# One core, linear attention and two gated layers: 160 orders from the planner, and leftover output sums moved amid the last up-projections

## The chip, the cores and the metric

The kernel runs on one core of one Trainium2 chip. The metric is device time in microseconds (us) of one execution; the lower, the better. The engines are called as in the profile: PE (TensorE), DVE (VectorE), ACT (ScalarE), POOL (GpSimd), SP (the engine whose queue issues the transfers).

## The reference

```
# attention: q, k, v are 4 batches x 8 heads x 576 rows x 64
q_s = softmax(q, over the 64)
k_s = softmax(k, over the 576 rows)
kv  = einsum('bhsd,bhse->bhde', k_s, v)
x   = einsum('bhsd,bhde->bhse', q_s, kv)      # then 2304 rows x 512
# layer 0 (2304 x 512, width 1536)
x = (silu(x @ w_gate) * (x @ w_val)) @ w_out
# layer 1, same sizes
out = ((x @ w_a) * (x @ w_b)) @ w_out2
```

All in float32. The kernel keeps that precision by splitting each operand of a product into a rounded high half and a low remainder and making three products (low x high, high x low, high x high) where the reference has one.

## The kernel before

**Stages.** In the first 140 us the attention of batches 0 and 1 runs together with layer 0 for the first block of 512 rows (block 0); the layer's twelve weight slices w_0 to w_11 are brought in and converted meanwhile (`convert`: the instructions of lines 390 to 416 on ACT, DVE and POOL, then a high half `w<-a` on ACT, line 416, and a low half `w<-a` on DVE or POOL, line 304). For slice f, PE makes 24 up-projection matmuls (`u_0_f`, line 837), and later 12 down-projections (`acc`, line 864) of the slice before. Attention works in units of two heads. A unit's matmuls on PE are `kx` (line 647) and `kb` (652), which take the maximum of the keys over the rows and spread it, `kv` (710, 711), `qt` (758), `ql` (761), `xt` (771) and `xl` (781); around them DVE finds maxima (`kr`, 650) and subtracts (`ut<-ut,kb`), ACT takes exponentials and copies `qt` to SBUF (765). Up to 293 us follows block 1 with the attention of batches 2 and 3, and from there the rest of both layers in three supersteps of six `step`s, which use a scheme in the manner of Strassen: seven products of half size in place of eight.

**A step** makes up-projections `p` (line 1115, six matmuls each, in `begin`, `middle` and `end` for m = 0 and 1), copies and gates their results (ACT lines 1127, 1131, 1153; DVE `temps<-p`), splits the gated tiles into `hs` (names hp and l2w in the rows, since they share those buffers), and makes output chunks `o` (`out_chunk`, lines 1226 and 1228, six matmuls each), whose results DVE adds into `sums`. Steps of the supersteps 0 and 2 also have the rows left over from the blocks: `rest_up` (`q`, line 1199, four results a step) and two more chunks, o_8 and o_9, added into `rs`. A step's chunks are not made in the step itself; they are `left` for the next. There, two of them go amid the m = 1 up-projections (in the loop with `end(1, which)`) and the others behind the `q` matmuls. The last step's own ten chunks come at the very end. The output weights of a step are split from `raww` into `outs_w` (`make_out`, ACT and DVE or POOL, lines 311 and 304). In the supersteps with rest rows this pair of buffers is the same in each step, so the split waits until the last chunk of the step before has been multiplied.

**The order.** No engine program is written by hand. `add` records every operation with its engines, cost in us, buffers and dependences. `prepare` gives each operation a due time, backwards from its successors, and `order` is a list scheduler: it takes the operation that can start first by its model of the engines, among those the one with the smallest due time, also picks DVE or POOL (or ACT or DVE) where an operation may go to either, and sets `self.length` to the end of its plan. `emit` then issues everything in that order, engine by engine; on the chip each engine keeps this order and waits in it. `soon` adds a chunk and gives its additions an early due time.

Of the kernel before, what the change touches and what calls it, by code (L numbers as in the profile page):

```python
# [1 line left out]

# [14 lines left out]
class Buf:  # L17
# [3 lines left out]
    def __init__(self, pool, shape, dtype, tag, name):  # L21
        self.pool, self.shape, self.dtype, self.tag, self.name = pool, shape, dtype, tag, name
        self.tile, self.users, self.seen, self.free = None, [], {}, False
# [7 lines left out]
class Plan:  # L31
# [13 lines left out]
    TABLE = 1.3  # L45
    WINDOW = 10.24 / 3
    FAR = 1e9

    def __init__(self):
        self.ops, self.last, self.rank = [], {}, {}  # L50
# [44 lines left out]
    def prepare(self):  # L95
# [7 lines left out]
        for n in reversed(range(len(ops))):  # L103
            op = ops[n]
            cost = op["cost"] + op["nbytes"] / self.DMA_RATE
            lands = (self.DMA_START + self.DMA_END) * (op["nbytes"] > 0)
            t = self.FAR
            for s in self.succ[n]:
# [9 lines left out]
    def order(self):  # L118
# [10 lines left out]
        def free_at(tag):  # L129
            if tag not in holder:  # L130
                return 0.0
            users = holder[tag].users
            return max(end[u] for u in users) + self.HOP if all(u in end for u in users) else self.FAR

# [6 lines left out]
        def port_at(n, engine):  # L141

            return max(port_free if e == engine and port else 0.0 for e, _, _, port in ops[n]["runs"])

        def better_here(n, r):

            (engine, cost, *_), (here, cost_here, *_) = ops[n]["runs"]
            queue = ready[engine]
            ahead = sum(ops[o]["cost"] for o in queue if due[o] < due[n] and queue[o] <= r + 1)
            return max(free.get(here, self.BEGIN), r, port_at(n, here)) + cost_here <= \  # L150
                max(free.get(engine, self.BEGIN), r, port_at(n, engine)) + ahead + cost
# [4 lines left out]
        while len(done) < len(ops):  # L156
            best = None
            for engine, queue in ready.items():
                options = []
                for n, r in queue.items():  # L160
# [3 lines left out]
                    for b in ops[n]["allocs"]:  # L164
                        r = max(r, min(free_at(tag) for tag in b.tag))
                    if r < self.FAR and (ops[n]["engine"] == engine or better_here(n, r)):
                        options.append((max(r, port_at(n, engine)), n))
# [44 lines left out]
        self.length = max(end.values())  # L212
        return done, run, slot

    def emit(self):
        self.prepare()
        done, run, slot = self.order()
        for b, tag in slot.items():
            b.tag = tag
        for n in done:  # L220
            self.ops[n]["runs"][run[n]][2]()
# [3 lines left out]
def kernel(  # L225
# [108 lines left out]
    NP = NF // 2  # L334
# [635 lines left out]
    def unit(u):  # L970
# [27 lines left out]
    SUMS = [((sums, k), lambda k=k: sums()[:, k]) for k in range(2 * R)] + \  # L998
        [((b, 0), lambda b=b: b()) for b in rest_sums]
    BANKS = ("at0", "at1", "acc2", "acc3")  # L1000
    SOON, SOONER, KEEP = 2.0, -30.0, 6
    main["soon"] = SOON
    SUPER = [(0, (2, 3), True, 512), (1, (0, 1), False, 512), (1, (2, 3), True, 512)]

    def bank(name):
        return Buf(pg, [P, 512], F32, BANKS, name)

    def parts(s):

        RAW, (l, blocks, _, width) = [*RAW1, *RAW2[s]] if s else [*RAW2[0], *RAW1], SUPER[s]  # L1010

        def cols(x):
            return x().rearrange("p (c n) -> p c n", c=2)[:, :, 0:width]

        for q, (t, h) in enumerate(((0, 0), (0, 1), (1, 0), (1, 1))):
            i = blocks[t]
            pieces = [(i, 0, width, 0)] if i < B else [(i - 1, width, SM - width, 0), (i, 0, B * SL, SM - width)]
            for src, at, size, to in pieces:
                last_x[:] = [dma(lambda q=q, h=h, src=src, at=at, size=size, to=to: nc.sync.dma_start(
                    out=RAW[q][1]().rearrange("p (c n) -> p c n", c=2)[:, :, to:to + size],  # L1020
                    in_=xd[l][src]()[:, 2 * h:2 * h + 2, at:at + size]),
                    P * 2 * size * 4, [(xd[l][src], (2 * h + c, 0)) for c in range(2)] if s == 0 else [xd[l][src]],
                    [(RAW[q][0][0], (RAW[q][0][1], to))], after=[*last_x, *(() if s or t == 0 else pair_buf["after"])])]

        def keys(q):
            return [(RAW[q][0][0], (RAW[q][0][1], to)) for to in ((0, SM - width) if blocks[q // 2] == B else (0,))]

        def halve(o, q):
            (hi_key, hi), (lo_key, lo) = ops_x[o]
            split(lambda: cols(hi), lambda: cols(lo), lambda: cols(RAW[q][1]), 2 * width, hi_key, lo_key, keys(q))  # L1030

        def less(q, x, y, op=ALU.subtract):
            pair(2 * width, lambda: cols(RAW[q][1]), lambda: cols(RAW[x][1]), lambda: cols(RAW[y][1]), op,
                 [*keys(x), *keys(y)], keys(q))

        halve(0, 0)
        less(0, 0, 2)
        less(2, 2, 3, ALU.add)
        halve(2, 2)
        halve(4, 0)  # L1040
        less(0, 3, 0)
        halve(1, 0)
        halve(3, 1)
        less(1, 1, 0)
        halve(5, 3)
        halve(6, 1)

    def rest_parts(l):
        last_x[:] = [dma(lambda: nc.sync.dma_start(
            out=RAW1[0][1]().rearrange("p (c n) -> p c n", c=KD), in_=xd[l][B]()),  # L1050
            P * PART * 4, [xd[l][B]], [(RAW1[0][0][0], (RAW1[0][0][1], 0))], after=[*last_x, *pair_buf["after"]])]
        (hi_key, hi), (lo_key, lo) = rest_x
        split(hi, lo, RAW1[0][1], PART, hi_key, lo_key, (RAW1[0][0][0], (RAW1[0][0][1], 0)))

    def step(s, j):
# [91 lines left out]

        p = [[Buf(pg, [P, 512], F32, (f"gv{m}",) if x == 1 else BANKS, f"p{n}_{m}_{x}") for x in range(3)] for m in range(2)]
        A, Bt = T
# [129 lines left out]
    def soon(chunk):  # L1279
        start = len(plan.ops)  # L1280
        chunk()
        for n in range(start, len(plan.ops)):
            if plan.ops[n]["engine"] in ("vector", "scalar"):
                plan.rank[n] = main["at"] + SOONER

    left, later = [], []
    for s, (l, _, rested, _) in enumerate(SUPER):
        parts(s)
        if rested:
            rest_parts(l)  # L1290
        for j in range(NP):
            begin, middle, end, rest_up, chunks, make_out = step(s, j)
            begin(0)
            while j == 0 and len(left) > KEEP:
                soon(left.pop(0))
            middle(0)
            begin(1)
            end(0, 0)
            end(0, 1)
            middle(1)  # L1300
            for which in range(2):
                if left:
                    soon(left.pop(0))
                end(1, which)
            for i in range(2 * rested):
                rest_up(i)
            for c in left:
                soon(c)
            for halve in later:
                halve()  # L1310
            later.clear()
            make_out()
            left = chunks
# [35 lines left out]
```

## Time and profile before

| | |
|---|---|
| median of 3 runs | 957.19 us (956.98 to 959.25) |
| profiled execution | 957.91 us, its span 955.5 us, mean granted PE clock 0.990 |
| busy share of the span | PE 96%, DVE 67%, ACT 54%, POOL 34% |

The span reaches from the first to the last instruction in the profile; the profiled execution's time is 2.4 us longer. PE is busy for 916.6 us of the span, and the other engines have room on average. A share of the span hides that the stages differ, so the stretches are read one by one.

### The profile page before, as it was taken

The page shows a single profiled execution, that of the slowest core. Times are in us where ns is not written, and L with a number is a line of the kernel's source. Part 1 is how long each engine was busy: PE and PEld are TensorE (multiplying, and loading weights), DVE is VectorE, ACT ScalarE, POOL GpSimd, SP SyncE. Part 2 cuts the span into 40 slices and gives each one's busy share as a digit, 9 for nine tenths or more (in the row PEclk, how much of TensorE's full clock was granted, in tenths as well). Part 3 has the DMA queues.
Part 4 walks back from the last instruction along what each step waited for, and adds up shares of the span by engine and source line. Part 5 has one row for each costly group of instructions (what it writes and reads, how often), then busy time and mean ns, then how long its engine had stood idle before and what let it go on. Part 6 is the DMA issues. An engine that isn't in the chain of part 4 may idle for free.

```text
span 955.5 us, 12768 instructions
## 1 busy us (share of the span) xinstructions
PE 916.6 (96%) x4400; PEld 755.8 (79%) x4400; DVE 641.9 (67%) x1029; ACT 519.2 (54%) x1020; POOL 325.2 (34%) x321
## 2 busy tenths in 40 slices
PE   5689899999999999999999999999999999999997
PEld 3477687877887888888888888888777888888885
DVE  7899897445377887867878775765686444564444
ACT  4797975877765665455454456443643453433311
POOL 6513211111124422343456333353464213242210
PEclk9899899999999999999999999999999999999999
DMA  9949675364337444453432652422223210110003
GB/s 269 290 165 283 216 223 188 115 193 123 84 102 254 131 134 153 130 157 122 143 111 69 207 188 88 135 90 84 67 65 108 83 44 23 45 45 23 23 1 110
DMA packets 108151, 121.41 MB, mean 127 GB/s; under 512 B 31928, under 2 KB 83896, under 8 KB 107960
## 3 DMA queue, kind: packets, MB, share of 16 engines
q1 hardware_dynamic: 102424, 116.55, 38.8%
q10 hardware_dynamic: 5664, 4.07, 1.4%
q8 instruction: 34, 0.56, 0.2%
q14 instruction: 29, 0.24, 0.1%
HBM read 88.60 MB, written 31.98 MB: 126 GB/s over the span
## 4 chain that ended last, share of the span: by engine, by line
PE 85%; DVE 6%; DMA 3%; ACT 2%; issue 2%; POOL 1%; SPq 1%; ACTq 0%; DVEq 0%; POOLq 0%
PE p L1115 34%; PE o L1226 14%; PE u L837 12%; PE q L1199 7%; PE o L1228 6%; PE acc L864 6%; PE o L1236 2%; DVE l2w L304 2%; PE kv L710 1%; DVE sums L304 1%; PE xt L771 1%; PE u L822 1%; DMA r<-x 1%; DMA wr<-in_moe_w_gate_dram 1%; DMA raw<-x 1%
## 5 line engine op out<-in xcount | busy, mean ns | idle before, releaser
L1115 PE MATMUL p<-l2w,l2w 128*128 128x512 f32 x1512 | 353.6, 390 | 3.2 <-ACT temps L1127 1.5
L1115 PEld LDWEIGHTS p<-l2w,l2w 128*128 128x128 f32 x1512 | 282.7, 188 | 64.8 <-DVE temps L304 2.9
L837 PE MATMUL u<-xhl,w 128*128 128x512 f32 x552 | 147.7, 414 | 3.9 <-DVE w L304 3.9
L837 PEld LDWEIGHTS u<-xhl,w 128*128 128x128 f32 x552 | 104.1, 195 | 29.5 <-DVE w L304 4.9
L311 ACT CAST l2w<-raww 128x512 fp32r<-128x512 f32 x144 | 88.2, 620 | 66.8 <-PE p L1115 35.2
L304 DVE TENSOR_TENSOR sums<-o,sums 128x512 f32<-128x512 f32 x120 | 82.2, 688 | 53.6 <-PE o L1226 38.4
L304 POOL TENSOR_TENSOR l2w<-raww,l2w 128x512 fp32r<-128x512 f32 x56 | 76.7, 1375 | 94.6 <-ACT l2w L311 92.8
L304 DVE TENSOR_TENSOR temps<-p,temps 128x512 f32<-128x512 f32 x90 | 62.1, 690 | 64.1 <-PE p L1115 63.3
L304 DVE TENSOR_TENSOR l2w<-raww,l2w 128x512 fp32r<-128x512 f32 x88 | 71.2, 820 | 31.8 <-ACT l2w L311 31.7
L1226 PE MATMUL o<-l2w,hp 128*128 128x512 f32 x288 | 82.4, 395 | 2.9 <-DVE sums L304 1.5
L864 PE MATMUL acc<-h,w 128*128 128x512 f32 x288 | 73.9, 400 | 0.0
L1127 ACT COPY temps<-p 128x512 f32<-128x512 f32 x72 | 42.4, 588 | 57.9 <-PE p L1115 57.3
L1226 PEld LDWEIGHTS o<-l2w,hp 128*128 128x128 f32 x288 | 53.3, 188 | 16.1 <-DVE sums L304 3.2
L1199 PE MATMUL q<-rest,l2w 128*128 128x256 f32 x432 | 65.4, 283 | 0.0
L864 PEld LDWEIGHTS acc<-h,w 128*128 128x128 f32 x288 | 52.9, 188 | 12.8 <-issue 0.8
L1199 PEld LDWEIGHTS q<-rest,l2w 128*128 128x128 f32 x432 | 58.6, 192 | 0.9
L311 ACT CAST l2w<-temps 128x512 fp32r<-128x512 f32 x36 | 22.3, 621 | 62.9 <-PE o L1226 47.8
L1226 PE MATMUL o<-l2w 128*128 128x512 f32 x192 | 54.6, 392 | 0.0
L304 POOL TENSOR_TENSOR raww<-raww,spare 128x512 f32<-128x512 f32 x15 | 20.8, 1385 | 86.1 <-DVE l2w L304 86.0
L1226 PE MATMUL o<-l2w,l2w 128*128 128x512 f32 x168 | 44.6, 391 | 0.0
L1228 PE MATMUL o<-hp,l2w 128*128 128x512 f32 x144 | 41.9, 399 | 1.3 <-DVE sums L304 1.2
L1226 PEld LDWEIGHTS o<-l2w 128*128 128x128 f32 x192 | 36.0, 188 | 8.3
(197 smaller groups left out, 1482.3 us busy)
## 6 DMA issues: line engine op xcount, KB each, us to landing
raww<-wf SPq DMA_DIRECT2D x36, 512.0 KB, 4.0
raww<-wf SPq DMA_DIRECT2D x36, 256.0 KB, 2.7
wf<-latewr SPq DMA_DIRECT2D x36, 256.0 KB, 3.1
wf<-a SPq DMA_DIRECT2D x16, 384.0 KB, 2.8
latewr<-in_moe_w_a_dram SPq DMA_DIRECT2D x24, 256.0 KB, 3.7
latewr<-in_moe_w_b_dram SPq DMA_DIRECT2D x24, 256.0 KB, 4.8
latewr<-in_moe_w_out_dram SPq DMA_DIRECT2D x12, 512.0 KB, 4.3
wr<-in_moe_w_gate_dram SPq DMA_DIRECT2D x22, 256.0 KB, 4.9
```

The lines of the kernel that those rows point to most:

```text
L304: engine.tensor_tensor(out=out(), in0=x(), in1=y(), op=op)
L311: add("scalar", act_us(n), lambda: nc.scalar.copy(out=hi(), in_=src()), src_keys, [hi_key])
L710: nc.tensor.matmul(pk(), lhsT=kx()[:, r, :], rhs=vx()[:, :, r, :], start=(r == 0), stop=False)
L771: add("tensor", 0.95, lambda: nc.tensor.matmul(px(), lhsT=kvbd(), rhs=qT()[:, 0:SM], start=True, stop=True), [QT, *BDS], [px], due=due)
L837: nc.tensor.matmul(ps()[:, 0:n], lhsT=wv[:, c, :], rhs=x()[:, xs, c, 0:n], start=(a == 0 and c == 0), stop=(a == 2 and c == KD - 1))
L864: nc.tensor.matmul(ps()[:, 0:n], lhsT=w()[:, 4 + ws, o * P:(o + 1) * P], rhs=h()[:, hs, 0:n], start=begin, stop=end)
L1115: nc.tensor.matmul(ps()[:, 0:width], lhsT=wv(o)[:, m, ws, c, :], rhs=ops_x[o][xs][1]().rearrange("p (c n) -> p c n", c=2)[:, c, 0:width], ...
L1127: add("scalar", act_us(n), lambda: nc.scalar.copy(out=to[1]()[:, 0:n], in_=ps()[:, 0:n]), [ps], [to[0]], due=main["at"] + main["soon"])
L1199: nc.tensor.matmul(ps[m]()[:, 0:256], lhsT=wv(o)[:, m, ws, c % 2, :], rhs=rest_x[xs][1]().rearrange("p (c n) -> p c n", c=KD)[:, c, :], st ...
L1226: nc.tensor.matmul(ps(), lhsT=lhs(i, hs), rhs=outs_w[i][1]()[:, ws * 512:(ws + 1) * 512], **ends)
L1228: nc.tensor.matmul(ps()[:, 0:width], lhsT=outs_w[i][1]()[:, ws * 512 + r * P:ws * 512 + (r + 1) * P], rhs=hs2[i][t][1]()[:, hs * 512:hs * ...
L1236: nc.tensor.matmul(ps()[:, o * 256:(o + 1) * 256], lhsT=outs_w[i][1]()[:, ws * 512 + at:ws * 512 + at + P], rhs=rest_h[1]()[:, (2 * i + hs ...
```

## The change

`search` runs `order` 160 times. From the second time on it first moves 3% of the due times by up to 3 us either way, and it keeps the moved due times where the plan's length does not grow. `emit` issues the last order kept. In the last step of superstep 2 (`EARLY[2]` is 1), chunks that were left over from the step before are added right behind `end(0, 0)` until four are left, and behind `end(0, 1)` until two are left; those two go in the loop as before, so none is left for behind the `q` matmuls.

```
+    ROUNDS = 160
+    def search(self):
+        self.prepare()
+        rng, best = random.Random(0), None
+        for n in range(self.ROUNDS):
+            kept = self.due
+            if best:
+                self.due = [d + rng.uniform(-3, 3) if rng.random() < 0.03 else d for d in kept]
+            try:
+                found = self.order()
+            except RuntimeError:
+                self.due = kept
+                continue
+            if best and self.length > best[0]:
+                self.due = kept
+            else:
+                best = self.length, found
+        return best[1]
...
     def emit(self):
-        self.prepare()
-        done, run, slot = self.order()
+        done, run, slot = self.search()
...
+    EARLY = (0, 0, 1)
...
             end(0, 0)
+            early = EARLY[s] if j == NP - 1 else 0
+            while early and len(left) > 4:
+                soon(left.pop(0))
             end(0, 1)
+            while early and len(left) > 2 * (early < 2):
+                soon(left.pop(0))
             middle(1)
```

In the rows of the changed program, lines stand 20 to 21 higher than before up to 1226 (304 is 324, 837 is 857, 1115 is 1136, 1226 is 1247).

**The last step, on PE.** Before, behind o16_0 (the first chunk left over from the step before) PE goes on like this, and only then to the `q` of the last step, number 17:

```order
L1226 MATMUL o16_0_7577<-l2w10_2926 128x512 x3
L1115 MATMUL p17_1_1_7540<-l2w5_2608,l2w8_2639 128x512 x6
L1226 MATMUL o16_1_7593<-l2w9_2686,hp0_2906 128x512 x3
L1226 MATMUL o16_1_7593<-l2w10_2926 128x512 x3
L1115 MATMUL p17_1_2_7533<-l2w6_2694,l2w8_2639 128x512 x6
L1199 MATMUL q17_0_0_7608<-rest2_2714,l2w9_2686 128x256 x2
L1199 MATMUL q17_0_0_7608<-rest2_2714,l2w7_2565 128x256 x2
```

Now the last chunks left over stand there:

```order
L1247 MATMUL o16_8_7642<-l2w9_2685,l2w6_2698 128x512 x3
L1247 MATMUL o16_8_7642<-l2w10_2919,l2w6_2698 128x512 x3
L1136 MATMUL p17_1_1_7540<-l2w5_2613,l2w8_2627 128x512 x6
L1247 MATMUL o16_9_7659<-l2w9_2685,l2w6_2698 128x512 x3
L1247 MATMUL o16_9_7659<-l2w10_2919,l2w6_2698 128x512 x3
L1136 MATMUL p17_1_2_7533<-l2w6_2698,l2w8_2627 128x512 x6
L1220 MATMUL q17_0_0_7680<-rest2_2719,l2w9_2685 128x256 x2
L1220 MATMUL q17_0_0_7680<-rest2_2719,l2w7_2565 128x256 x2
```

Eight chunks have moved from behind the 48 `q` matmuls to ahead of them. Behind the last `q` the step's own chunks now follow at once:

```order
L1220 MATMUL q17_1_1_7728<-rest2_2719 128x256 x2
L1220 MATMUL q17_1_1_7728<-rest2_2719,l2w8_2627 128x256 x2
L1220 MATMUL q17_1_1_7728<-rest2_2719 128x256 x2
L1220 MATMUL q17_1_1_7728<-rest2_2719,l2w8_2627 128x256 x2
L1247 MATMUL o17_0_7743<-l2w9_2685,hp0_2897 128x512 x3
L1247 MATMUL o17_0_7743<-l2w10_2919 128x512 x3
```

**The last step, on ACT.** Before, these are its last instructions but two; `l2w9` and `l2w10` from `raww` are the high halves of the last step's output weights, `tr` is the gate of `q`:

```order
L1127 COPY temps_2800<-p17_1_1_7540 128x512
L1131 ACTIVATE tr_2963<-q17_0_0_7608 128x256
L1131 ACTIVATE tr_2963<-q17_1_0_7637 128x256
L311 CAST hp0_2906<-tc_2822 128x512
L311 CAST l2w10_2926<-temps_2800 128x512 x2
L311 CAST hp1_2946<-temps_2800 128x512
L311 CAST l2w9_2686<-raww_1910 128x512
L311 CAST l2w10_2926<-raww_1910 128x512
```

Now the same instructions stand in this order:

```order
L331 CAST hp0_2897<-tc_2818 128x512
L331 CAST l2w10_2919<-temps_2798 128x512
L331 CAST hp1_2941<-temps_2798 128x512
L331 CAST l2w9_2685<-raww_1907 128x512
L331 CAST l2w10_2919<-raww_1907 128x512
L1152 ACTIVATE tr_2957<-q17_0_0_7680 128x256
L331 CAST l2w10_2919<-temps_2798 128x512
```

The casts of hp0, l2w10, hp1 and of the output weights (`<-raww`) have moved ahead of the first `tr<-q`.

**The first step of superstep 2, on ACT.** Before, the cast of the rest rows (`rest2<-r1`, whose rows arrive by a transfer) stands ahead of the gate and of the copy of `p12_1_1`, for which PE's next up-projection waits:

```order
L1127 COPY temps_2800<-p12_1_2_6148 128x512
L311 CAST rest2_2714<-r1_2538 128x1024
L1131 ACTIVATE temps_2800<-p12_0_1_6082 128x512
L311 CAST l2w8_2639<-raww_1910 128x2x256
L311 CAST l2w9_2686<-raww_1910 128x2x256
L1127 COPY temps_2800<-p12_1_1_6155 128x512
```

Now:

```order
L1148 COPY temps_2798<-p12_1_2_6147 128x512
L1152 ACTIVATE temps_2798<-p12_0_1_6083 128x512
L331 CAST rest2_2719<-r1_2538 128x1024
L331 CAST l2w8_2627<-raww_1907 128x2x256
L1148 COPY temps_2798<-p12_1_1_6154 128x512
```

The gate `temps<-p12_0_1` has moved ahead of the cast of the rest rows, and one of the two casts of `raww` behind the copy of `p12_1_1`.

**Block 0, on PE, around slice 6.** Before, unit 6's `kb` and unit 7's `kx` stand between the down-projections and the up-projections of slice 7:

```order
L864 MATMUL acc0_2_550<-h0_0_5_984,w0_5_810 128x512 x3
L864 MATMUL acc0_3_556<-h0_0_5_984,w0_5_810 128x512 x3
L652 MATMUL kb6_1059<-ident_78,kr6_1004 128x128
L647 MATMUL kx7_1078<-ident_78,tm7_1018 128x128 x2
L647 MATMUL kx7_1078<-ident_78,ut7_829 128x128
L837 MATMUL u0_0_7_0_1089<-xhl0_0_286,w0_7_1036 128x512 x12
L837 MATMUL u0_0_7_1_1128<-xhl0_0_286,w0_7_1036 128x512 x12
```

Now unit 6's `kx` and `kb` come ahead of slice 5's up-projections:

```order
L667 MATMUL kx6_876<-ident_78,tm6_823 128x128 x2
L667 MATMUL kx6_876<-ident_78,ut6_702 128x128
L730 MATMUL kv5_886<-ut5_473 128x130 x4
L731 MATMUL kv5_886<-ut5_473 128x130
L672 MATMUL kb6_897<-ident_78,kr6_892 128x128
L857 MATMUL u0_0_5_0_913<-xhl0_0_299,w0_5_835 128x512 x12
```

And between slices 6 and 7 there is no attention any more:

```order
L884 MATMUL acc0_0_550<-h0_0_5_995,w0_5_835 128x512 x3
L884 MATMUL acc0_1_558<-h0_0_5_995,w0_5_835 128x512 x3
L884 MATMUL acc0_2_564<-h0_0_5_995,w0_5_835 128x512 x3
L884 MATMUL acc0_3_572<-h0_0_5_995,w0_5_835 128x512 x3
L857 MATMUL u0_0_7_0_1113<-xhl0_0_299,w0_7_1037 128x512 x12
L857 MATMUL u0_0_7_1_1131<-xhl0_0_299,w0_7_1037 128x512 x12
```

Two matmul groups of attention that stood right ahead of `u0_0_7` are gone from there.

**Block 0, on DVE, up to the second half of w_6.** Before, the low halves of w_6 are made here:

```order
L406 SCALAR_TENSOR_TENSOR a0_6_1_925<-wr0_6_1_812,a0_6_1_925 128x768
L411 ISA a0_6_1_925<-wr0_6_1_812,a0_6_1_925 128x1536
L304 TENSOR_TENSOR w0_6_953<-a0_6_0_859,w0_6_953 128x3x256
L851 TENSOR_TENSOR u0_0_5_1_927<-s0_0_5_932,u0_0_5_1_927 128x512
L304 TENSOR_TENSOR w0_6_953<-a0_6_1_925,w0_6_953 128x3x256
L397 TENSOR_SCALAR a0_7_0_977<-a0_7_0_977 128x768
```

Now there is more between and ahead of them:

```order
L417 TENSOR_SCALAR a0_6_1_943<-a0_6_1_943 128x768
L324 TENSOR_TENSOR w0_6_959<-a0_6_0_884,w0_6_959 128x3x256
L420 TENSOR_SCALAR a0_6_1_943<-a0_6_1_943 128x768
L871 TENSOR_TENSOR u0_0_5_1_954<-s0_0_5_964,u0_0_5_1_954 128x512
L426 SCALAR_TENSOR_TENSOR a0_6_1_943<-wr0_6_1_825,a0_6_1_943 128x768
L431 ISA a0_6_1_943<-wr0_6_1_825,a0_6_1_943 128x1536
L417 TENSOR_SCALAR a0_7_0_990<-a0_7_0_990 128x768
L324 TENSOR_TENSOR h0_0_5_995<-u0_0_5_1_954,h0_0_5_995 128x512
L420 TENSOR_SCALAR a0_7_0_990<-a0_7_0_990 128x768
L735 TENSOR_SCALAR ks6_1017<-kv6_1002 128x2
L426 SCALAR_TENSOR_TENSOR a0_7_0_990<-wr0_7_0_908,a0_7_0_990 128x768
L324 TENSOR_TENSOR w0_6_959<-a0_6_1_943,w0_6_959 128x3x256
```

The second low half, `w0_6<-a0_6_1`, now stands behind work on slice 7, behind `h0_0_5` and, further ahead, behind unit 6's `kr6` and its two subtractions of `kb6` and behind `tm7`, all of which came after it before.

## Rows read from the trace of the kernel before

**Rows 1.** Windows: length, busy of PE, PEld, DVE, ACT, POOL, PE clock, DMA, GB/s

```profile
24.00:50.00 26.00, 18.41 (x76) 13.54 (x75) 22.76 (x36) 20.19 (x42) 14.02 (x18) 0.87 0.92 297
...
100.00:125.00 25.00, 21.81 (x88) 17.16 (x87) 21.02 (x35) 22.31 (x49) 7.90 (x7) 0.86 0.66 213
...
300.00:900.00 600.00, 594.05 (x2904) 497.87 (x2903) 403.13 (x600) 292.80 (x520) 234.31 (x166) 1.00 0.32 102
```

**Rows 2.** Timeline of PE, 88 to 126 us: start, duration, what, idle before

```profile
90.78 1.16 PE L710 MATMUL kv<-ut 128*128 128x130 f32 x8 [1.39 <-ACT ut L765]
...
101.65 5.74 PE L837 MATMUL u<-xhl,w 128*128 128x512 f32 x24
107.22 2.96 PE L864 MATMUL acc<-h,w 128*128 128x512 f32 x12
...
112.61 0.44 PE L647 MATMUL kx<-ident,tm 128*128 128x128 f32 x2 [2.31 <-DVE ut L304]
...
114.50 8.02 PE L837 MATMUL u<-xhl,w 128*128 128x512 f32 x22 [0.88 <-DVE w L304]
122.36 2.26 PE L864 MATMUL acc<-h,w 128*128 128x512 f32 x9
124.46 1.05 PE L710 MATMUL kv<-ut 128*128 128x130 f32 x8
```

**Rows 3.** Timeline of DVE, 100 to 113 us

```profile
100.03 0.95 DVE L304 TENSOR_TENSOR w<-a,w 128x768 fp32r<-128x768 f32 x1
100.90 0.55 DVE L397 TENSOR_SCALAR a<-a 128x768 f32<-128x768 f32 x1
101.37 0.68 DVE L304 TENSOR_TENSOR h<-u,h 128x512 fp32r<-128x512 f32 x1
101.97 0.55 DVE L400 TENSOR_SCALAR a<-a 128x768 uint32<-128x768 uint32 x1
102.44 0.55 DVE L650 TENSOR_REDUCE kr<-kx 128x1 f32<-128x384 f32 x1
102.91 0.94 DVE L406 SCALAR_TENSOR_TENSOR a<-wr,a 128x768 uint32<-128x768 uint32 x1
103.77 0.41 DVE L304 TENSOR_TENSOR tm<-ut 128x256 f32<-128x256 f32 x1
...
110.33 0.69 DVE L304 TENSOR_TENSOR ut<-ut,kb 128x512 f32<-128x512 f32 x1
...
112.27 0.28 DVE L304 TENSOR_TENSOR ut<-ut,kb 128x128 f32<-128x128 f32 x1
```

**Rows 4.** Timeline of PE at the first step of superstep 2

```profile
722.38 1.65 PE L1115 MATMUL p<-l2w,l2w 128*128 128x512 f32 x6 [1.49 <-ACT temps L1127]
```

**Rows 5.** Timeline of ACT at the same place

```profile
719.27 1.05 ACT L311 CAST rest<-r 128x1024 fp32r<-128x1024 f32 x1 [3.14 <-DMA r<-x]
720.22 0.59 ACT L1131 ACTIVATE temps<-p 128x512 f32<-128x512 f32 x1
...
721.74 0.58 ACT L1127 COPY temps<-p 128x512 f32<-128x512 f32 x1
```

**Rows 6.** Timeline of PE in the last step

```profile
918.39 3.04 PE L1199 MATMUL q<-rest,l2w 128*128 128x256 f32 x24
...
924.15 0.85 PE L1226 MATMUL o<-l2w,hp 128*128 128x512 f32 x3
...
936.76 0.97 PE L1226 MATMUL o<-l2w,hp 128*128 128x512 f32 x3 [1.38 <-DVE l2w L304]
```

**Rows 7.** Timeline of ACT in the last step

```profile
934.74 1.30 ACT L311 CAST l2w<-raww 128x512 fp32r<-128x512 f32 x2 [1.08 <-PE o L1226]
```

**Rows 8.** Timeline of DVE in the last step

```profile
936.03 1.28 DVE L304 TENSOR_TENSOR l2w<-raww,l2w 128x512 fp32r<-128x512 f32 x2
```

**Rows 9.** The page's groups of instructions: the same subtraction on POOL and DVE

```profile
L304 POOL TENSOR_TENSOR l2w<-raww,l2w 128x512 fp32r<-128x512 f32 x56 | 76.7, 1375 | 94.6 <-ACT l2w L311 92.8
...
L304 DVE TENSOR_TENSOR l2w<-raww,l2w 128x512 fp32r<-128x512 f32 x88 | 71.2, 820 | 31.8 <-ACT l2w L311 31.7
```

More of the change, by code (lines that the diff above doesn't have):

```diff
@@ L1 @@
+import random
 from contextlib import ExitStack
```

## The prediction

> **What bounds the kernel now.** I read the windows first. They give, for each stretch, how long each engine was busy, and the reader should compare PE's busy time with the stretch's length. From 300 to 900 us PE is busy for 594.05 of 600 us [rows 1]: PE sets the pace, and an edit there can win only single waits. From 24 to 50 us it is busy for 18.41 of 26 us, from 100 to 125 us for 21.81 of 25, and the granted clock is 0.87 and 0.86 there: part of the matmuls ran at 1.2 GHz instead of 2.4. In these stretches DVE is busy for 22.76 of 26 and 21.02 of 25 us. So the front is bound by the conversion of the weight slices on DVE and ACT, with PE waiting for it, and the rest is bound by PE.
>
> Then the timelines of PE, in which square brackets give the idle time before a row and what ended it. Three places can be touched by the change. In the front, PE waits 2.31 us for unit 7's `kx` and 0.88 us for the low half of w_7; the 22 matmuls behind take 8.02 us, 0.365 us each, where 24 like them took 5.74 us, 0.239 each [rows 2]. The difference, 22 x 0.126 = 2.8 us, is the low clock after the waits. At 722 us PE waits 1.49 us for a copy on ACT [rows 4]. At 936.76 it waits 1.38 us for the last step's output weights [rows 6].
>
> **The last step: -1.4 us.** The number of matmuls is the same; eight chunks are only moved ahead of `q`. Before, ACT could cast the output weights only at 934.74, behind the last leftover chunk, whose buffers they take [rows 7]; DVE took their low halves from 936.03 [rows 8], and PE waited 1.38 us. Now the leftover chunks end ahead of `q`, and `q` lasts from 918.39 to 924.15, 5.76 us [rows 6]. The two casts (1.30 us together) and two subtractions (1.28 on DVE, or 1.375 for the one that POOL now has [rows 9]) fit into it: at the worst one behind the other 1.30 + 1.28 + 1.38 = 4.0 us. All of the 1.38 us goes if nothing else is late. What is late next is the low half of the last gated tile: behind the last up-projection DVE has an addition and a multiplication, ACT a cast, DVE a subtraction, and in the new order the cast stands behind `tr<-q17_0_0`, the subtraction behind the multiplication for `q17_0_1`. `q17_0_1` is the second of four and ends half of `q` later, at 2.9 us; with some 0.7 us for each of the two DVE instructions behind it the low half is there at about 4.3 us, 1.5 us before it is needed. What the eight chunks displace in the up-projections is covered: each is 1.4 us of PE (924.15 to 936.76 less the wait is eight of them: 11.2 us) and leaves DVE one addition of 0.7 us. The ends are -1.4 and 0; I take -1.4.
>
> Beside it stands a row against that slack: the same subtraction takes 820 ns on DVE over 88 of them [rows 9], and 640 ns a piece in the pair at 936.03 [rows 8], so something stretches it in places. The Trainium skill, page "SBUF — State Buffer", section "Who interferes with whom", says that a DVE instruction with two SBUF inputs and a GpSimd instruction that reads SBUF lock each other out. The trace agrees in direction (a mean above the undisturbed pair); POOL has four such subtractions or products in the last step now, and by that rule the last low half could be up to one POOL instruction, 1.4 us, later, at 5.7 us against 5.8. That would still give -1.4 us, but with the slack gone; it is part of why the third rival below is not left out.
>
> **The first step of superstep 2: -0.8 us.** ACT waited for the transfer of the rest rows until 719.27, then ran their cast, 1.05 us, the gate, two casts and only at 721.74 the copy [rows 5]. PE had nothing to do from 722.38 - 1.49 = 720.89 [rows 4], when the copy's input was ready. Now the gate runs in ACT's wait for the transfer, and one cast of 0.6 us goes behind the copy. So the copy could start at 721.74 - 0.59 - 0.57 = 720.6; it starts when its input is there, at about 720.95, and 0.8 us is saved. Ends: 0 if the transfer lands later than before, -1.5 if the rest of the wait goes as well. I take -0.8.
>
> **The front: -0.5 us.** Around slice 6 the new orders of PE and DVE pull unit 6's `kx` and `kb` ahead of slice 5, and its `kv` ahead of slice 6. That has a price: the second half of w_6 on DVE now stands behind eight further instructions of some length. Six of them followed it directly before, from 100.90 to 104.18, 3.3 us; the two subtractions of `kb` are 0.69 and 0.28 [rows 3]. So w_6 is complete at 100.03 + 0.95 + 4.2 = 105.2, and `u0_6` starts there instead of at 101.65. If the clock stays high, it ends at 110.9, the 2.96 us of `acc` end at 113.9, and `u0_7` starts when w_7 is there. That came at 114.5 before [rows 2]; DVE has much the same work ahead of it, only in another order, and I put it at 115.0. Then `u0_7` takes 5.74 us at full clock, without the wait of 2.31 us for `kx`, and ends at 120.7; before, it ended at 122.36. That is -1.7 us. If the wait of 3 us ahead of `u0_6` lowers the clock, as it was low behind the waits at 112.61 and 114.50, 2.8 us are added there: 113.7, `acc` 116.7, `u0_7` 122.4, no change. Two more moves belong to this: `kv` of unit 6, 1.05 us at 124.46, now runs in the wait ahead of `u0_6`, and `xt` of unit 6 now stands right behind `qt` and `ql`, so that it waits for ACT's copy of `qt`; the nearest such wait is 1.39 us at 90.78 [rows 2]. Together +0.3. So -1.4 to +0.3; I take -0.5, near the middle. From there to 140 us both orders do the same slices, and I carry it on unchanged. Before slice 5 the new order moves DVE's and ACT's work too, to and fro; I have no row that tells which way it goes and put nothing there.
>
> **The rest: +0.5 us.** In block 1 and behind it, PE's rows are shuffled as well, mostly attention among up-projections, where PE has almost no idle time, so it can hardly gain. A `kb` moved nearer to its `kx` or a `kv` nearer to its `kb` makes a wait. The bounds are 0 and one wait of 2.31 us such as `kx` had [rows 2]. I take +0.5, nearer to 0, since most distances are kept.
>
> **Sum.** -0.5 + 0.5 - 0.8 - 1.4 = -2.2 us. The profiled execution took 957.91 us (span 955.5 and 2.4 us around it), so it would take 955.7, its span 953.3. It lies 0.7 us above the median of the runs; the same step from 957.19 gives 955.0 us.
>
> **Rivals.**
> - *The front gains in earnest.* For it speaks that PE lost 3.2 us of waits and 2.8 us of clock between 112 and 122 us, and that DVE itself is idle for 4 of the 25 us from 100 to 125 us [rows 1], so that w_6 and w_7 could come sooner than my count of rows says. If the front gained those 4.0 us, the sum is -4.0 + 0.5 - 0.8 - 1.4 = -5.7: 951.5 us by the median. Against it speaks the longer line ahead of w_6.
> - *Slower, by w_6.* If `u0_6` starts at 105.2 at the low clock and the clock stays low through all 24 matmuls and the 12 of `acc`, these take 24 x 0.365 + 12 x 0.365 = 13.1 us instead of 8.5; `u0_7` starts at 118.3 instead of 113.7. With its own half of 5.74 us at the low clock as well (+1.5), it ends at 125.5, 3.1 us behind before. With the wait at `xt`, +0.3, and the rest at its bound, +2.3, the front and the middle cost 5.7 us; less 2.2 us behind, +3.5: 960.7 us. It decides if `u0_7` ends after about 125 us. That PE's clock rises with its own activity and is otherwise held down is what the Trainium skill, page "TensorE: Matmul & The Clock Gate", section "What's actually happening", says too; the low rate behind the waits at 112.61 and 114.50 agrees.
> - *Nothing real.* The last step's wait is only replaced (the low half of the last gated tile, or a leftover chunk that now waits for its input among the up-projections, -0.4 instead of -1.4), the copy at 722 us waits for a later transfer (0), and front and middle cancel: -0.4, within the spread of the runs, 956.8 us.
>
> **How the numbers follow.** Chances: my sum 0.47, the first rival 0.20, the second 0.16, the third 0.17. The bound between a change and none, 0.3%, is 2.9 us: 954.3 and 960.1. The sum's own range is from -4.4 (front -1.4, rest 0, -1.5, -1.5) to +1.0 (front +0.3, rest +1.5, the other two half), that is 952.8 to 958.2; I give 0.20 of its 0.47 to below 954.3. The first rival is faster; of the second three quarters are slower; the third is no change. Faster: 0.20 + 0.20 = 0.40; slower 0.12; the same 0.27 + 0.04 + 0.17 = 0.48. The range has to take in the first rival's 951.5 and most of the second: 951 to 960.
>
> **What would show it.** In the last step no wait of PE ahead of the own chunks, and the output weights' casts ahead of the first `tr<-q`. At about 720 us the gate ahead of the cast of the rest rows, and a wait of 0.7 us or less in place of 1.49. In the front, `u0_6` late by some 3.5 us behind a wait for DVE's w, no wait of `kx` ahead of `u0_7`, `u0_7` ending between 120.7 and 122.4 us. I am wrong if the windows from 24 to 100 us, where I put nothing, show PE's busy time moved by more than 2 us or the low clock in other places, or if block 1 shows several new waits.

## The result, and the profile after

The changed kernel takes 946.93 us (median of 6 runs, 945.76 to 948.39) against 957.0 us of before in the same measurements; the ratio is 0.9895, 95% interval 0.9883 to 0.9907. It is 10 us faster where 2 were forecast, and lies outside the range of 951 to 960. The profiled execution has a span of 945.2 us, 10.3 less than before.

Where the time came from is read first from two marks on PE. The up-projections of the steps begin at 289.14 us in place of 293.63, so 4.5 us come from the front. Behind the first wait of the steps both kernels still have 3,096 matmuls to issue; that stretch lasts 644.6 us before (310.9 to 955.5) and 638.8 after (306.4 to 945.2), so 5.8 us come from there. These are single profiles: the runs below whose order there is that of before (e1, e4, e5, e11, e12) have 642.3 to 643.8 us for the same stretch, so the times of whole runs have to confirm the split.

The windows of the changed kernel that answer to [rows 1]:

```profile
24.00:50.00 26.00, 17.53 (x70) 12.54 (x69) 23.04 (x39) 19.33 (x30) 13.78 (x19) 0.81 0.87 278
100.00:125.00 25.00, 22.32 (x104) 17.64 (x103) 24.07 (x38) 21.19 (x45) 4.54 (x3) 1.00 0.76 241
300.00:900.00 600.00, 596.81 (x2922) 501.55 (x2922) 402.81 (x602) 293.89 (x521) 232.72 (x165) 1.00 0.33 102
```

From 100 to 125 us PE's clock is full, and DVE is busy for 24.07 us in place of 21.02. From 24 to 50 us PE has no more work done than before, and from 24 to 100 us its busy time is 65.7 us in place of 64.2, which stays under the 2 us that the prediction named as a sign of being wrong. The timeline of PE from 100 us, in answer to [rows 2]:

```profile
101.40 1.05 PE L730 MATMUL kv<-ut 128*128 128x130 f32 x8
...
102.43 0.71 PE L857 MATMUL u<-xhl,w 128*128 128x512 f32 x2
105.03 5.32 PE L857 MATMUL u<-xhl,w 128*128 128x512 f32 x22 [1.89 <-DVE w L324]
110.19 2.96 PE L884 MATMUL acc<-h,w 128*128 128x512 f32 x12
112.99 5.67 PE L857 MATMUL u<-xhl,w 128*128 128x512 f32 x24
118.50 1.79 PE L884 MATMUL acc<-h,w 128*128 128x512 f32 x7
```

Slice 6 waits for its weights until 105.03 (the forecast was 105.2), slice 7 does not wait and ends at 118.50, where the forecast was 120.7 to 122.4 and before 122.36.

The first step of superstep 2, timelines of ACT and PE, in answer to [rows 4, 5]: the gate runs ahead of the cast of the rest rows, and PE has no wait at all in its up-projections.

```profile
710.65 0.60 ACT L1152 ACTIVATE temps<-p 128x512 f32<-128x512 f32 x1 [0.72 <-PE p L1136]
712.33 1.05 ACT L331 CAST rest<-r 128x1024 fp32r<-128x1024 f32 x1 [1.08 <-DMA r<-x]
...
714.18 0.58 ACT L1148 COPY temps<-p 128x512 f32<-128x512 f32 x1
```

```profile
704.78 11.69 PE L1136 MATMUL p<-l2w,l2w 128*128 128x512 f32 x49
716.31 0.86 PE L1247 MATMUL o<-l2w,hp 128*128 128x512 f32 x3
```

The last step, in answer to [rows 6 to 8], timelines of PE, ACT and DVE:

```profile
920.85 3.04 PE L1220 MATMUL q<-rest,l2w 128*128 128x256 f32 x24
...
926.60 0.85 PE L1247 MATMUL o<-l2w,hp 128*128 128x512 f32 x3
```

```profile
919.63 1.14 ACT L331 CAST l2w<-raww 128x512 fp32r<-128x512 f32 x2
```

```profile
921.77 1.44 DVE L324 TENSOR_TENSOR temps<-temps 128x512 f32<-128x512 f32 x1
923.13 0.68 DVE L324 TENSOR_TENSOR l2w<-raww,l2w 128x512 fp32r<-128x512 f32 x1
...
924.33 0.68 DVE L324 TENSOR_TENSOR l2w<-temps,l2w 128x512 fp32r<-128x512 f32 x1
```

The step's own chunks follow `q` at 926.60 without a wait. The output weights are cast before `q` begins, and the last low half is there at 924.33 + 0.68 = 925.0, 1.6 us ahead of its need (forecast: 1.5).

The waits of PE from 300 to 940 us, before and after (in total, times, longest):

```profile
PE o L1226 <- DVE sums L304: 1.5, 4, 0.9
PE p L1115 <- ACT temps L1127: 1.5, 1, 1.5
PE o L1226 <- DVE l2w L304: 1.4, 1, 1.4
PE o L1228 <- DVE sums L304: 1.2, 3, 0.7
PE p L1115 <- DVE temps L304: 1.0, 2, 0.8
PE p L1115 <- DVE l2w L304: 0.6, 1, 0.6
```

```profile
PE o L1249 <- DVE sums L324: 1.6, 4, 1.0
PE p L1136 <- DVE temps L324: 1.1, 2, 0.8
PE o L1247 <- DVE sums L324: 0.2, 1, 0.2
```

7.2 us became 2.9. PE's busy time in the stretch of 3,096 matmuls fell as well, from 633.46 to 631.79 us: some of that is the slow start behind a wait (three matmuls of `o` behind one take 0.97 us, others 0.85). For about 1 us of it I have no row; part of that is scatter, since the profiles with the order of before have 632.6 to 633.1 us.

### The profile page after: what moved, and what is told of

Its sections match the earlier page's. It is cut to its first block, busy times and chain, and to the rows that moved or that the text cites. A ratio compares the mean times of both kernels' runs of the same rounds, so it can differ in the third digit from the quotient of the medians.

```text
span 945.2 us, 12797 instructions
## 1 busy us (share of the span) xinstructions
PE 913.9 (97%) x4400; PEld 755.7 (80%) x4400; DVE 641.7 (68%) x1025; ACT 519.2 (55%) x1020; POOL 331.9 (35%) x323
## 4 chain that ended last, share of the span: by engine, by line
PE 80%; DVE 8%; DMA 6%; ACT 3%; issue 2%; SPq 1%; POOL 0%; DVEq 0%; ACTq 0%
PE p L1136 34%; PE o L1247 15%; PE u L857 9%; PE q L1220 7%; PE o L1249 6%; PE acc L884 5%; PE o L1257 2%; DVE l2w L324 1%; PE kv L730 1%; DMA wr<-in_moe_w_gate_dram 1%; PE xt L791 1%; DVE sums L324 1%; DMA wr<-in_moe_w_out_dram 1%; DMA wf<-a 1%; DMA raww<-wf 1%
## 5 line engine op out<-in xcount | busy, mean ns | idle before, releaser
L857 PE MATMUL u<-xhl,w 128*128 128x512 f32 x552 | 143.9, 408 | 5.0 <-DVE w L324 4.7
L324 POOL TENSOR_TENSOR l2w<-raww,l2w 128x512 fp32r<-128x512 f32 x68 | 97.0, 1431 | 97.9 <-ACT l2w L331 97.8
L857 PEld LDWEIGHTS u<-xhl,w 128*128 128x128 f32 x552 | 102.2, 192 | 31.8 <-DVE w L324 6.8
L324 DVE TENSOR_TENSOR l2w<-raww,l2w 128x512 fp32r<-128x512 f32 x76 | 55.6, 742 | 26.6 <-ACT l2w L331 26.5
L496 POOL TENSOR_TENSOR latewr<-latewr 128x512 uint32<-128x512 uint32 x17 | 23.9, 1410 | 63.5 <-DVE latewr L491 47.9
```

What stands on the lines that cost most here:

```text
L324: engine.tensor_tensor(out=out(), in0=x(), in1=y(), op=op)
L496: engine.tensor_tensor(out=u32(), in0=u32(), in1=r()[..., 0], op=ALU.add)
L857: nc.tensor.matmul(ps()[:, 0:n], lhsT=wv[:, c, :], rhs=x()[:, xs, c, 0:n], start=(a == 0 and c == 0), stop=(a == 2 and c == KD - 1))
```

## The experiments

All keep the computation but the last two, and are timed against runs of before on the same chip. The search leaves moved due times in 1,571 of 3,479 operations. They can be given to one single order as a table, and the table can be cut at a time of the plan:

```
+MOVED = {0: -2.8554, ...}          # operation: change of its due time
...
+        self.prepare()
+        for n, by in MOVED.items():
+            self.due[n] += by
+        return self.order()
```

**e1, e2: the first cut.** The table of the search cut at 150 us, its first part without `EARLY`, its second with it.

```
e1: MOVED: 302 entries planned before 150 us;  EARLY = (0, 0, 0)
e2: MOVED: 1269 entries planned behind 150 us; EARLY = (0, 0, 1)
```

> Only the due times that the search moved for operations of the first 150 us (302 of 1571) are moved; the last step is issued as before. Theory A, the gains of the change stand in separate places and add up: block 1 began 4.5 us sooner in the changed kernel, so this kernel is 4.5 us faster than before, 952.5 us (951.5 to 953.5), with no wait of 2.3 us for kx and PE's clock at 1.00 from 100 to 125 us. Rival B, a gain in the front is given back where later operations wait for DVE: 955.5 us or more.

> Only the due times of the operations behind the first 150 us are moved (1269), and the last step is issued as in the change. Theory A: what is left of the 10.1 us when the front's 4.5 us are missing, 5.6 us, so 951.4 us (950.4 to 952.4); the waits of 2.3 and 0.9 us in the front are as before. Rival B: the whole 10 us or nearly, 948 us, if the later moves alone carry it.

Measured: e1 958.58 us, ratio 1.0017 (1.0008 to 1.0027), slower; e2 957.25 us, 1.0004 (0.9993 to 1.0014), no change. In e1 rival B held, and the loss was more than the gain; in e2 neither theory did. The profiles say why. In e1 the matmuls of slice 7 behind its first two begin at 113.86 us, with a wait of 0.18 only, yet the gain is lost at slice 11, where PE waits for DVE's w (timelines of PE and DVE of e1):

```profile
154.85 0.62 PE L848 MATMUL u<-xhl,w 128*128 128x512 f32 x2
157.53 6.86 PE L848 MATMUL u<-xhl,w 128*128 128x512 f32 x22 [2.06 <-DVE w L315]
```

```profile
156.52 0.96 DVE L315 TENSOR_TENSOR w<-a,w 128x768 fp32r<-128x768 f32 x1 [0.23 <-ACT w L427]
```

Behind that wait the 22 matmuls take 6.86 us, at a granted clock of 0.75 from 157.5 to 164.4 us, where those of e5 below take 5.29. My cut had gone through the conversion of w_11, whose last pieces are planned behind 150 us. In e2 the steps begin at 300.87 us, 7.2 later than before, but the stretch behind (318.2 to 957.1, 638.9 us) is as short as in the changed kernel. So the later gain does not need the front's.

**e3: the early chunks, no search.**

```
-    ROUNDS = 160
+    ROUNDS = 1
```

> One order (no search), with the leftover chunks issued amid the last up-projections. Theory A: the wait for the output weights goes (1.4 us) and little else: 955.5 us (954.5 to 956.5). Rival B: the new due times of the last step shuffle the rest of the kernel too, and the sum may come out either way by 2 us or more, 953 or 958 us.

Measured: 956.97 us, ratio 1.0 (0.999 to 1.001). Neither time came, but rival B's mechanism is what the profile shows: due times are counted backwards from the end, so the edit of the last step moved due times all over the kernel and with them the order from slice 8 on. w_11 is complete at 158.57 us, the steps begin at 297.33, 3.7 us later than before; behind 314.6 us the stretch takes 640.2 us, 4.4 less than before and 1.8 less than in e7 below, which holds the edit of the last step alone. So a part of the later gain can come without any search, from the shift of the due times.

**e4: unit 6's keys first.**

```
+MOVED = {406: -20, 407: -20, 408: -20, 409: -20, 410: -20, 411: -20, 412: -20, 413: -20}
```

> As before, but the due times of eight operations, those from tm6 to the subtraction of kb6 in attention unit 6, are 20 us earlier; no search, the last step as before. Theory A, it is the lateness of kb6 that made kx7 wait 2.3 us and brought the low clock: u0_7 ends at 119 us or sooner and the kernel is 3 to 4.5 us faster, 953.3 us (952.5 to 954). Rival B, the front is bound by DVE's conversion and needs the other moved operations too: u0_7 ends at 121 to 123 us and the kernel is at most 1.5 us faster, 955.5 to 957 us.

Measured: 959.87 us, ratio 1.0034 (1.0022 to 1.0045), slower, which neither theory had. `kx7` waits no more, but `qt` waits 3.09 us in its place at 116.51 us, `u0_7` ends at 124.2 us, and w_11 is complete at 159.2 us. Taking away the wait that I had looked at gains nothing by itself.

**e5, e6, e7: cuts that keep each part whole.** Here the due times of a part are those of the changed kernel or of before as they stand, so that an edit at the end moves nothing ahead of it. In the orders, PE's order of e5 is that of the changed kernel up to the last step, and e7 agrees with before in all rows of all engines up to the last steps.

```
e5: before 294 us as changed, behind as before;  EARLY = (0, 0, 0)
e6: before 294 us as before,  behind as changed; EARLY = (0, 0, 1)
e7: all but the last steps as before;            EARLY = (0, 0, 1)
```

> The first 294 us of the plan take the due times of the changed kernel, all later operations those of before, and the last step is issued as before. Theory A, the front has two chains, PE's attention and up-projections, and the conversion of the weights whose last piece is w_11, and both had to come sooner: w_11 is complete at about 153.3 us, the first step's up-projections begin at about 289 us and the kernel is 4.5 us faster than before, 952.2 us (951.5 to 953). Rival B, 955.5 us or more: the front's gain is given back behind it.

> The first 294 us take the due times of before, all later operations those of the changed kernel, and the last step is issued as in the change. Theory A, the parts stand apart: first up-projections of the steps at 293.6 us, and 5.8 us are gained behind them, 951 us (950.3 to 952). Rival B, the later order gains only with its own front before it: 954 us or more.

> All operations ahead of the last steps keep the due times of before; only the leftover chunks are issued amid the last up-projections. Theory A, the wait of 1.38 us for the output weights goes and nothing else moves: 1.4 to 1.9 us faster, 955.0 us. Rival B, the wait comes back at another place of the last step: no change, 956.5 us or more.

Measured: e5 951.5 us, ratio 0.9949 (0.9932 to 0.9965); e6 950.93 us, 0.9936 (0.9922 to 0.995); e7 955.45 us, 0.9984 (0.9973 to 0.9995). Theory A in all three: the parts stand apart. In e5 slice 11 finds its weights (timelines of PE and DVE of e5), and the steps begin at 289.29 us:

```profile
151.81 0.62 PE L848 MATMUL u<-xhl,w 128*128 128x512 f32 x2
152.65 5.29 PE L848 MATMUL u<-xhl,w 128*128 128x512 f32 x22 [0.22 <-DVE w L315]
```

```profile
151.64 0.95 DVE L315 TENSOR_TENSOR w<-a,w 128x768 fp32r<-128x768 f32 x1
```

**e8: the later part without the last step.** As e6, with `EARLY = (0, 0, 0)`. PE's order is that of before in all its 4,272 matmuls.

> Only operations planned behind 294 us take the due times of the changed kernel, the front keeps those of before, and the last step is issued as before. PE's order is that of before in every row; DVE, ACT, POOL and the transfers differ. Theory A: what the later half gained without its tail, 6.0 less 1.4, 4.6 us: 952.2 us (951.3 to 953), with fewer waits of PE for DVE's sums and for the copy at 722 us. Rival B, the gain needs the new last step: 955.5 us or more.

Measured: 952.76 us, ratio 0.9955 (0.9941 to 0.9969). Theory A. With PE's order untouched, 4.3 us (957.0 x 0.0045) come from the order of the other engines and of the transfers. The waits of PE from 300 to 940 us:

```profile
PE o L1238 <- DVE l2w L315: 2.2, 2, 1.4
PE p L1127 <- DVE l2w L315: 1.2, 2, 0.6
PE p L1127 <- DVE temps L315: 0.8, 1, 0.8
PE o L1240 <- DVE sums L315: 0.2, 1, 0.2
```

The waits for `sums` have gone from 2.7 to 0.2 us and that for ACT's copy is gone; two short ones for weights are new. One of the waits for `sums` that are gone is seen in the timelines of PE and DVE, before:

```profile
699.84 0.97 PE L1226 MATMUL o<-l2w,hp 128*128 128x512 f32 x3 [0.89 <-DVE sums L304]
```

```profile
696.86 2.32 DVE L304 TENSOR_TENSOR r<-r2wr,r 128x1024 f32<-128x1024 f32 x1
699.10 1.27 DVE L304 TENSOR_TENSOR sums<-o,sums 128x512 f32<-128x512 f32 x2
```

and in e8:

```profile
696.45 1.40 DVE L315 TENSOR_TENSOR sums<-o,sums 128x512 f32<-128x512 f32 x2
698.87 0.69 DVE L315 TENSOR_TENSOR sums<-o,sums 128x512 f32<-128x512 f32 x1 [1.02 <-PE o L1238]
699.48 1.79 DVE L315 TENSOR_TENSOR r<-r2wr,r 128x1024 f32<-128x1024 f32 x1
```

A preparation of 2.32 us stood ahead of two sums for which PE waited 0.89 us at 699.84; now it stands behind them.

**e9: one cast moved.** The term of 0.8 us by itself: the cast of the rest rows behind the gate, PE's rows all as before.

```
+MOVED = {2853: 15.0}
```

One neighbouring pair on DVE changes places with it: the low half of the rest rows now stands behind a `temps<-p`.

> As before, but the due time of one operation, the cast of the rest rows in the first step of superstep 2, is 15 us later: on ACT it stands behind the gate, everything else is as before. Theory A, the step of the prediction: 0.8 us faster, 956.0 us, PE's wait at 722 us 0.7 us instead of 1.49. Rival B, the whole of this wait and the one after it go, as in the changed kernel: 1.5 to 1.8 us faster, 955.2 us. Rival C: no change, the transfer or a cast still holds the copy.

Measured: 956.05 us, ratio 0.9997 (0.9988 to 1.0006): too small to be told from no change; 0.8 lies within the interval, rival B's 1.5 to 1.8 outside. In its profile PE's wait is 0.76 us, as theory A has it (PE and ACT), and the next wait, 0.25 us at 725.65 before, is gone too:

```profile
721.22 1.66 PE L1127 MATMUL p<-l2w,l2w 128*128 128x512 f32 x6 [0.76 <-ACT temps L1139]
```

```profile
718.25 1.05 ACT L322 CAST rest<-r 128x1024 fp32r<-128x1024 f32 x1 [1.23 <-DMA r<-x]
```

But this wait changes from one execution to the next with the order on ACT as before. It is 1.49 us in the profile of before, 1.11 in e1, 1.25 in e4, 1.06 in e7, 0.84 in e11, 0.22 in e12 (timeline of PE) and none in e5:

```profile
720.40 1.66 PE L1115 MATMUL p<-l2w,l2w 128*128 128x512 f32 x6 [0.22 <-ACT temps L1127]
```

From the start of the rest rows' cast to that of the copy it is 2.34 us in e9 (718.25 to 720.59) and 2.47 before (719.27 to 721.74), so this order brought 0.1 us there. The other 0.6 are the transfer, which ACT waited for until 718.25, 2.2 us ahead of PE's coming to a stop, and before until 719.27, 1.6 us ahead of it.

**e10: a longer search.** The changed kernel's due times, and 1,500 orders more by the same rule.

> The change with the due times that 1500 further orders of the same search keep. Theory A, what the search sees as shorter is shorter on the chip, and another 1 to 4 us go: 944.5 us (943 to 946). Rival B, what is left to the search lies within what the chip does otherwise from run to run, and nothing is gained: 946.5 us or more.

Measured: 947.01 us, ratio 0.9899 (0.9885 to 0.9913), as the change; a gain of about 1 us is not excluded. Rival B: in its profile the steps begin at 287.38 us, 1.8 sooner than in the change, but the median of the four runs does not show it. No version beat the change. The planner's own count (`self.length` of the order that is issued) is 964.7 us for before, 961.1 for the change and 950.3 here: it saw 3.6 of the 10 us, and then 10.8 us that the chip does not show.

**e11, e12: less conversion.** The clamp of line 397, which holds magnitudes between two bounds of the kernel (`LEAST` and `TOP`), is left out for slices 8 to 11, in e1 and in before; no other row moves.

```
-        add("vector", dve_us(size, 2), lambda: nc.vector.tensor_scalar(
+        add("vector", dve_us(size, 2), lambda: f < 8 and nc.vector.tensor_scalar(
```

> The kernel of the first experiment (the moved due times of the first 150 us alone), without one DVE instruction of the conversion, the clamp of line 397, in slices 8 to 11: eight instructions of 0.55 us, 4.4 us of DVE. Nothing else differs in any engine's order. Theory A, the front ends when the conversion of w_11 does: w_11 is complete some 4 us sooner, PE's wait for it goes, the steps begin at 290 to 292 us in place of 296, and the kernel takes 953.5 us (952.5 to 955). Rival B, PE's new waits for attention between slices 7 and 9 (1.15, 0.83 and 0.97 us) are what costs: 957 us or more.

> The kernel before without the same eight instructions in slices 8 to 11. Theory A, two chains that end together: PE's own, with its waits and low clock at slice 7, reaches slice 11 at 157 us as before, so that 4.4 us less for DVE gain little: 0 to 1.5 us, 955 to 956.5 us. Rival B, the conversion alone bounds the front: 3.5 us or more, 953 us or less.

Measured: e11 954.58 us, ratio 0.9977 (0.9967 to 0.9987), where e1 had 1.0017, so 3.8 us less; e12 956.18 us, ratio 1.0001 (0.9992 to 1.001). Theory A by the times of both, though in e11 w_11 comes 2.5 us sooner and not 4, and PE's wait for it falls from 2.06 to 1.59 us only; another 1.6 us are the clock, since the 22 matmuls behind take 5.29 us again. Lightening the conversion gives e1 what it had lost, though its waits for attention are still there (0.88, 0.32 and 1.44 us), and gives the kernel before nothing. There w_11 came only 1.0 us sooner. DVE spent what it had saved in waiting, most of it for ACT's high halves of w; its waits from 100 to 157 us, before and in e12:

```profile
DVE w L304 <- ACT w L416: 0.4, 1, 0.4
```

```profile
DVE w L304 <- ACT w L416: 4.2, 4, 2.6
```

The times that decide, from the timelines of DVE and PE (us):

| | PE's first matmul of slice 11 | w_11 complete | steps begin |
|---|---|---|---|
| before | 156.95 | 157.46 | 293.63 |
| changed | 152.49 | 153.28 | 289.14 |
| e1 | 154.85 | 157.48 | 296.04 |
| e2 | 156.54 | 159.77 | 300.87 |
| e3 | 155.34 | 158.57 | 297.33 |
| e4 | 156.60 | 159.18 | 298.26 |
| e5 | 151.81 | 152.59 | 289.29 |
| e9 | 156.33 | 156.83 | 293.57 |
| e11 | 152.87 | 155.03 | 291.96 |
| e12 | 156.31 | 156.42 | 293.27 |

The steps begin 136 to 139 us behind the later of the two, and 141 in e2, where PE waits another 2.8 us in block 1. The first row, in the timelines of PE and DVE of before:

```profile
156.95 5.89 PE L837 MATMUL u<-xhl,w 128*128 128x512 f32 x24
```

```profile
156.51 0.95 DVE L304 TENSOR_TENSOR w<-a,w 128x768 fp32r<-128x768 f32 x1
```

## Why the prediction was wrong

**The last step, -1.4: right.** e7, which holds nothing else, is 1.5 us faster (0.5 to 2.6), and the wait, the order and the slack are those of the working. On DVE `temps<-temps` took 1.44 us at 921.77 beside POOL's subtraction at 921.37, where the subtraction of the same size at 923.13, with POOL idle, took 0.68; the slack held. The Trainium skill, page "SBUF — State Buffer", section "Who interferes with whom", says that a DVE instruction with two SBUF inputs contends with a GpSimd instruction that reads SBUF, and this row agrees.

**The first step of superstep 2, -0.8: the wait went, but its mechanism is shown only in part.** In the changed kernel the 1.49 us and the 0.25 behind them are gone, 1.7 us; the end of -1.5 stood in the working. From the start of the rest rows' cast to that of the copy it is 1.85 us there (712.33 to 714.18) in place of 2.47, so the new order on ACT brought 0.6 of the 0.8. The cast itself began 4.0 us ahead of PE's next `o` (712.33 and 716.31), where before it began 4.6 us ahead, of which 1.5 were the wait (719.27 and 723.87); so the transfer landed about 0.9 us sooner against PE. The working took that landing from one profile. It differs between executions by more than the whole term (1.49 us to none in the runs named under e9), and in e8, where the cast still stands ahead of the gate, the rest rows had landed in time and PE did not wait either. What the term is worth in the time of a run stays open.

**The front, -0.5: the step that failed.** It was right for slice 6, to 0.2 us. It failed in "I put it at 115.0" for w_7: its last piece was there at 112.23 + 1.10 = 113.3 us on DVE, slice 7 began at 112.99 without a wait, ran at the full clock and ended at 118.50, 3.9 us sooner than before, where the working had 1.7 at best. The sentence "From there to 140 us both orders do the same slices, and I carry it on unchanged" held in number (4.5 us sooner at slice 11 and at the steps), but without its reason: a lead at slice 7 lasts only if the conversion of w_8 to w_11 comes sooner as well, and that the working did not follow.

Two chains run there side by side, PE's and the conversion, and in the kernel before they meet within half a microsecond (156.95 and 157.46). e9 shows it without any edit, since its order in the front is that of before on every engine: slice 7 ran at the full clock there and ended 2.2 us sooner, and PE lost most of that in a wait for w_8 (timeline of PE of e9):

```profile
115.03 5.28 PE L848 MATMUL u<-xhl,w 128*128 128x512 f32 x22 [0.89 <-DVE w L315]
...
126.44 1.65 PE L848 MATMUL u<-xhl,w 128*128 128x512 f32 x6 [1.31 <-DVE w L315]
```

e1 brought PE to slice 11 2.1 us sooner, with w_11 as late as before, and lost; e4 took one wait from PE, got another, and w_11 came 1.7 us later; e12 lightened the conversion and gained nothing; the changed kernel and e5 brought both chains 4 to 5 us forward, and their steps begin 4.5 and 4.3 us sooner. e5 alone is 4.9 us faster than before (3.3 to 6.5).

The windows fit: DVE stood still less, and POOL did more. From 24 to 150 us, before and after:

```profile
24.00:150.00 126.00, 110.24 (x487) 87.31 (x486) 112.97 (x171) 102.03 (x195) 37.40 (x47) 0.93 0.72 232
```

```profile
24.00:150.00 126.00, 113.02 (x507) 88.97 (x506) 117.82 (x177) 103.99 (x200) 42.30 (x50) 0.95 0.74 238
```

DVE's idle time fell from 13.0 to 8.2 us, by 4.8, and w_11 came 4.2 us sooner. In the lists of DVE's waits of that stretch, the two largest of before are gone and down to 0.6 us:

```profile
DVE ut L304 <- PE kb L652: 2.6, 3, 1.2
DVE a L397 <- ACT a L390: 2.5, 2, 1.5
```

```profile
DVE a L417 <- ACT a L410: 0.6, 1, 0.6
```

I counted what stood ahead of w_6 on DVE, not where DVE would wait. The first rival named this, with DVE's 4.0 us of idle time and a chance of 0.20; its price for the front holds (4.5 measured), and its sum of 951.5 us missed since it took the rest from my terms.

**The rest, +0.5: failed too.** "PE has almost no idle time, so it can hardly gain" took 594.05 of 600 us for nothing, but 6 us idle and the slow starts behind each wait were more than all I forecast. e8 took 4.3 us (3.0 to 5.6) from there without touching PE's order, the wait of the first step of superstep 2 among them. I had looked at how attention is shuffled on PE, not at the order of DVE, where preparations stood ahead of sums.

**The sum.** The upper end of the sum's own range, +1.0, adds up to +0.7 by its terms, which changes nothing here. e5, e8 and e7 multiply to 0.9949 x 0.9955 x 0.9984 = 0.9888, within the interval of the change. The parts add up. Which of some 950 moved due times behind 294 us brings how much, beyond the rows shown, and how much of it the search brings and how much the shift by the edit of the last step (e3), stays open. That 160 orders of this search came upon 10 us is in part luck: by the planner's count they were worth 3.6.

## What to carry to other kernels

Where two chains run side by side to a common point, follow both to that point: an edit that moved only one of them gained nothing here, and a wait taken away at one place showed up at another. In a stage that one engine seems to fill, list that engine's waits and their releasers over the whole stage; many small ones, with the slow start behind each, can be worth more than the one that an edit is about. With a scheduler that counts backwards from the end, a local edit can move the order everywhere, so to measure it the other operations have to be held where they were.

## What the runs showed of the hardware

Behind the same waits ahead of slice 7 (2.31 and 0.88 or 0.89 us), 22 matmuls took 8.02 us in the profile of before and 5.28 us in that of e9, whose order on every engine is the same there; the granted clock from 100 to 125 us was 0.86 and 1.00. So the lower of the two clocks came in one execution and not in the other. The steps began at 293.63 and 293.57 us, so the 2.7 us of clock did not set the end: PE waited 1.31 us for w_8 at 126.44 in e9, and not at all for it in the profile of before.

A DVE instruction of 128x1024 from two tiles in SBUF, `r<-r2wr`, took 2.32 us at 696.86, with POOL at work from 695.51 to 700.28 us without a gap, and 1.21 us at 506.23, where POOL was idle from 504.1 to 507.5. The rule of the Trainium skill named above, page "SBUF — State Buffer", section "Who interferes with whom", fits both rows.
